# A fused attention and feed-forward kernel: a score tile that waits for two more exponentials, and a planner that keeps TensorE in attention for work that is nearly ready

## The chip, the cores and the metric

The kernel runs on one core of a Trainium2 chip. The metric is the device time of one execution in microseconds (us), less is better. Three runs of the kernel before took 1133.21, 1135.22 and 1140.99 us, so its median is 1135.22.

Names used below: PE is TensorE (matmuls), DVE is VectorE, ACT is ScalarE, POOL is GpSimd, SP is the engine that issues most of the DMAs (transfers).

## The reference

Block-causal attention over q, k and v (8 batches, 8 heads, 576 positions of 64 features, blocks of 64 positions), then a feed-forward net without an activation function: two projections, multiplied element by element, and a third one.

```python
scores = q @ k.T / sqrt(64)                 # [576, 576] of each head
scores = where(row_block >= column_block, scores, -1e9)
attn = exp(scores - rowmax);  attn /= attn.sum() + 1e-09
x = heads side by side of (attn @ v)        # 4608 tokens x 512
out = ((x @ w_a) * (x @ w_b)) @ w_out       # 512 -> 1536 -> 512
```

All of it is in 32-bit floats. The later part of the kernel and the attention of most heads make a product of 32-bit precision out of three products of a rounded part and a rest ("hi" and "lo").

## The kernel before, in words

**Stages.** Attention works on 32 pairs of heads (pair p, counted from 0; four pairs make a batch). While the pairs run, the first third of the feed-forward net (hidden blocks 0 to 3) is computed for the batches that are done, so that PE has work where attention waits for other engines. Then come the last batch's share of that first third (function `rest`), and at last the other two thirds for all tokens (lines from 1077 on, matmuls of L1160), with weights that DVE and ACT convert meanwhile.

**One pair.** The steps carry names that recur below.
- `lk`, `lq`, `lv`: SP loads k, q and v. From pair 10 on, `kh` and `qh` (ACT, L512 and L504) round k and q to a hi part, `kl` (POOL) and `ql` (DVE, L508) make the rest. Pairs 0 to 9 use the plain 32-bit matmul.
- Scores: there are four tiles of 128 query rows, numbered 3, 2, 1, 0, and a "side" tile of the first and last block of keys. `C3` writes tile 3 into bank pair x (128x512 for each of the two heads). `C1` writes the side tile (128x128) and tile 1 (128x320) into bank pair y. `C2` writes tile 2 (128x448) into x again, when tile 3's exponentials `e3` have read x. `C0` writes tile 0 (128x192) into y again, when `e4` (the side tile) and `e1` (tile 1) have read y. All of them are matmuls of L542, on halves of the array (64 rows of weights).
- DVE masks and takes row maxima (`m`, `t` with the tile's number: L576 to L580 and L568), ACT takes the exponentials (`e`, L595), two a tile, one for each head.
- `rc` sums and inverts (DVE), `N` scales (POOL, L683), `T` transposes on DVE (L688, L693); pairs 0 to 5 transpose on PE instead (L709). `D`, 16 small DMAs (L739), gathers the transposed probabilities into the tile `at`. `V0` to `V3` multiply them by v (L748), `X` copies the result out of PSUM, `H` and `S` split it into hi and lo for the feed-forward net, which can start on a batch when its four pairs have got that far.
- The next pair's `C3` needs x, so it waits for `e2`; its `C1` needs y, so it waits for `e0`.

**What sets the order.** None of this is issued in the order in which it is written. Each step is an `Op` with an engine, a list of steps that it needs, a key (its due time) and a cost from the table `TOOK`. The function `plan` plays the engines through these costs, and at each turn takes the ready step with the lowest key; the instructions are then recorded in the order that came out, and every engine works through its own list in that order. The feed-forward work is cut into groups of four matmuls (`mm4`, 128x288 each) with the highest key, so it fills what attention leaves. Each step of PE has a mode: 0 for whole-array work (feed-forward groups, transposes), 1 for scores, 2 for the values. A step whose mode isn't that of the step before it costs the planner `SWITCH` more. `SLACK` (0.3 us) is added where PE waits for another engine. The second third of the work is planned by a second call of `plan`, whose steps all have mode 0.

Of the kernel before, what the change touches and what calls it, by code (L numbers as in the profile page):

```python
# [35 lines left out]
K2 = 2  # L36
FIRST = 8
WARM_P = 2
PET = 6
A_KEY = 12  # L40
SLOTS = [12.0] * 12 + [15.2] * 20
CONV_AT = [0, 6.8, 13.6, 20.4, 28.2, 36, 43.8, 51.6, 59.4, 67.2, 75, 82.8]
CONV_KEY = 12.0
CONV_LO = True
KEEP_UNTIL, KEEP_EVERY = 66.0, 2.5
SWITCH = 0.1
LAGS = {"PE": 0.24, "DVE": 0.14, "Activation": 0.17, "Pool": 0.1, "SP": 2.0}
TOOK = {
# [41 lines left out]
def attention_then_bilinear_ffn(  # L90
# [272 lines left out]
    PE_, DVE_, ACT_, POOL_, SP_ = LAGS  # L363
# [12 lines left out]
    def plan(look=0.0):  # L376
        free = dict.fromkeys(LAGS, 0.0)
        ready = {e: [] for e in LAGS}
        users = [[] for _ in ops]
        left = [len(o.deps) for o in ops]  # L380
        for o in ops:
            for d, plus in o.deps:
                users[d.n].append((o, plus))
            if not o.deps:
                ready[o.eng].append(o)
        out = []
        mode = 0
        bus = 0.0
        held = []

        def since(o):
            if not o.frees:
                return o.at
            if len(held) < MM:
                return o.at
            r = held[-MM]
            return o.at if r is o else 1e9 if r.end is None else max(o.at, r.end)

        while any(ready.values()):
            t, e = min((max(free[e], min(map(since, q))), e) for e, q in ready.items() if q)  # L400
            o = min((o for o in ready[e] if since(o) <= t + look), key=lambda o: (o.key, o.n))
            t = max(t, since(o))
            if o.frees:
                held.append(o.frees)
            ready[e].remove(o)
            free[e] = t + o.took + (SWITCH if e == PE_ and o.mode != mode else 0)
            if e == PE_:
                mode = o.mode
            if o.also:
                free[ACT_] = max(free[ACT_], t) + o.also  # L410
            o.start, o.end = t, free[e] + o.lag
            if o.kind in KB:
                bus = max(bus, t + LATENCY - 0.3) + KB[o.kind] / RATE
                o.end = bus + 0.3
            out.append(o)
            for u, plus in users[o.n]:
                u.at = max(u.at, o.end + plus + (SLACK if u.eng == PE_ and e != PE_ else 0))
                left[u.n] -= 1
                if not left[u.n]:
                    ready[u.eng].append(u)  # L420
        assert len(out) == len(ops)
        return out
# [40 lines left out]
    def attention(p):  # L463
# [90 lines left out]

        def c1():
            y = bank("y")
            scores(NT, y[:, :, side])
            scores(1, y[:, :, :nk[1]])

        add("C3", PE_, lambda: scores(LAST, bank("x")), [("ql", p), ("kl", p), ("e3" if single_next else "e2", p - 1)], 0, at=B0, mode=1, kind=nat + "C3")  # L560
        add("C1", PE_, c1, [("C3", p, -LAGS[PE_]), ("ql2", p), *([("e4", p - 1), ("e1", p - 1)] if single_next else [("e0", p - 1)])], 0.1, mode=1, kind=nat + "C1")
# [58 lines left out]
        if single:  # L620
            c1_ = ("C1", p, -LAGS[PE_])
            r2 = Op("none", PE_, lambda: ring(2, 0), [(got("C1", p), -LAGS[PE_])], key=B0 + K2)

            def c2():
                ring(2, 1)
                scores(2, [view(2, h) for h in range(2)])

            o2 = add("C2", PE_, c2, [(r2, 0.0), c1_], K2 + .01, mode=1, kind=nat + "C2")
            def c0():
                ring(0, 1)  # L630
                st[0, 0] = ps_sc.tile([P, 512], F32, tag="av", name=f"s{n}_0_0")
                scores(0, [view(0, h) for h in range(2)])

            o0 = add("C0", PE_, c0, [("C2", p, -LAGS[PE_]), ("X", p - 1)], K2 + .1, mode=1, kind=nat + "C0")
            add("t2", DVE_, lambda: [nc.vector.tensor_reduce(st["nm"][:, h, 2:3], view(2, h), axis=AX.X, op=ALU.max, negate=True) for h in range(2)], [("C2", p), ("t3", p)], K2 + 1, kind="u2")
            add("t0", DVE_, lambda: [nc.vector.tensor_reduce(st["nm"][:, h, :1], view(0, h), axis=AX.X, op=ALU.max, negate=True) for h in range(2)], [("C0", p), ("t3", p)], K2 + 1.2, kind="u0")
        else:
            add("C2", PE_, lambda: scores(2, bank("x")[:, :, :nk[2]]), [("e3", p), ("C1", p, -LAGS[PE_])], 7.0, mode=1, kind=nat + "C2")
            add("C0", PE_, lambda: scores(0, bank("y")[:, :, :nk[0]]),
                [("C2", p, -LAGS[PE_]), ("e1", p), ("e4", p)], 7.1, mode=1, kind=nat + "C0")  # L640
            if masked:
                done["m2", p] = got("C2", p)
            else:
                add("m2", DVE_, lambda: mask(2, "x"), [("C2", p)], 8.0)
            add("t2", DVE_, lambda: top(2, st["x"][:, :, :nk[2]]), [("m2", p)], 8.1)
            if masked:
                done["m0", p] = got("C0", p)
            else:
                add("m0", DVE_, lambda: mask(0, "y"), [("C0", p)], 8.2)
            add("t0", DVE_, lambda: top(0, st["y"][:, :, :nk[0]]), [("m0", p)], 8.3)  # L650
# [907 lines left out]
```

## Time and profile before

| | |
|---|---|
| median of 3 runs | 1135.22 us (1133.21 to 1140.99) |
| span of the profiled execution, first to last instruction | 1131.4 us |
| what the median has above that span | 3.8 us |
| PE, DVE, ACT, POOL busy | 1106.5, 867.4, 634.7, 407.0 us |
| attention with the feed-forward work among it | from 0 to some 540 us of the span |

The profiled execution's own time is not among the three; its span is known, and 3.8 us stands for what lies around it.

In the page, a row of a group gives line, engine, operation, the tile written and the tiles read, shape, count, and then busy time and the mean of one instruction. In the rows of the timeline, the first number is the start in us from the span's start, the second the time that the merged instructions took, then engine, line, operation and tiles; square brackets hold the idle time before them and what ended it. A matmul's own time is longer than its distance to the next one, since matmuls are pipelined: what a step of PE costs is read from one start to the next.

### The profile page before, as it was taken

Reading aid. Unit: us, or ns where it says so; the run is one execution under the profiler, and the core shown is the slowest. Engines: PE = TensorE matmul, PEld = TensorE weight load, DVE = VectorE, ACT = ScalarE, POOL = GpSimd, SP = SyncE. Lnnn points to the kernel's source line nnn. Section 1 sums busy time; section 2 is a strip of 40 time slices with the busy share of each in tenths; the row PEclk is TensorE's granted clock in tenths of the full one; section 3 lists DMA queues with packets and bytes.
Section 4 is the critical chain, followed back from the end, with each engine's and each line's share of the span. In section 5 each row is a group of like instructions: output and inputs, shape, how many; then the busy total and the mean of one; then the engine's idle time right before and its main releaser. Section 6 shows DMA issues by size and latency. Waiting matters only on the chain.

```text
span 1131.4 us, 23204 instructions
## 1 busy us (share of the span) xinstructions
PE 1106.5 (98%) x8441; PEld 1040.2 (92%) x8441; DVE 867.4 (77%) x1797; ACT 634.7 (56%) x1632; POOL 407.0 (36%) x602
## 2 busy tenths in 40 slices
PE   8899999999999999999999999999999999999998
PEld 5567888899989998999999999999999999999998
DVE  6877878687678777753999997787874867867857
ACT  6877576566666556643465554545543545545532
POOL 4876667566656667551100120211202112022020
PEclk9999999999999999999999999999999999999999
DMA  5542688888777877857242663845669135055151
GB/s 171 156 145 87 168 242 217 226 227 213 205 222 210 223 210 201 240 159 209 90 146 73 181 179 86 215 121 144 181 217 333 37 76 112 17 96 102 26 98 56
DMA packets 78257, 178.74 MB, mean 158 GB/s; under 512 B 13120, under 2 KB 34624, under 8 KB 78144
## 3 DMA queue, kind: packets, MB, share of 16 engines
q1 hardware_dynamic: 65472, 159.95, 47.2%
q0 software_dynamic: 12672, 17.31, 10.2%
q8 instruction: 67, 1.10, 0.4%
q14 instruction: 46, 0.38, 0.1%
HBM read 80.74 MB, written 48.76 MB: 114 GB/s over the span
## 4 chain that ended last, share of the span: by engine, by line
PE 78%; DVE 6%; DMA 5%; ACT 4%; POOL 3%; SPq 3%; issue 2%; DVEq 0%; ACTq 0%; POOLq 0%
PE bank L1160 47%; PE ps L261 13%; PE pso L261 6%; PE av L748 5%; PE x L542 3%; PE y L542 2%; SPq L739 2%; ACT e L595 2%; POOL e L683 1%; DMA at<-bl 1%; DVE bl L688 1%; DMA qr<-qT 1%; DVE nm L568 1%; PE tp L709 1%; DMA kr<-kT 1%
## 5 line engine op out<-in xcount | busy, mean ns | idle before, releaser
L1160 PE MATMUL bank<-xh,wab 128*128 128x384 f32 x1344 | 350.0, 338 | 0.7 <-DVE t L1077 0.7
L1266 POOL DMA_DIRECT2D outT<-pt x88 | 78.0, 1129 | 468.6 <-ACT pt L1413 277.6
L1160 PEld LDWEIGHTS bank<-xh,wab 128*128 128x128 f32 x1344 | 244.7, 187 | 1.4 <-DVE t L1077 1.0
L1160 PE MATMUL bank<-xl,wab 128*128 128x384 f32 x672 | 227.0, 338 | 0.0
L261 PE MATMUL ps<-xh,wab 128*128 128x288 f32 x1024 | 213.9, 298 | 0.4 <-ACT ob L873 0.3
L261 PEld LDWEIGHTS ps<-xh,wab 128*128 128x128 f32 x1024 | 165.8, 188 | 6.4 <-issue 4.3
L683 POOL TENSOR_SCALAR e<-e,rc 128x512 f32<-128x512 f32 (+3 forms) x256 | 152.7, 616 | 45.3 <-DVE rc L663 45.3
L261 PE MATMUL ps<-xl,wab 128*128 128x288 f32 x512 | 153.3, 299 | 0.0
L1160 PEld LDWEIGHTS bank<-xl,wab 128*128 128x128 f32 x672 | 125.9, 187 | 0.0
L1077 DVE TENSOR_TENSOR u<-bank,u 128x384 f32<-128x384 f32 x156 | 86.7, 556 | 48.4 <-PE bank L1160 45.2
L688 DVE STREAM_TRANSPOSE bl<-e 128x512 f32<-128x512 f32 (+1 forms) x208 | 110.2, 582 | 10.4 <-POOL e L683 8.7
L1160 PE MATMUL bank<-hz,wo 128*128 128x384 f32 x612 | 110.0, 334 | 0.0
L1160 PEld LDWEIGHTS bank<-hz,wo 128*128 128x128 f32 x612 | 106.5, 188 | 0.0
L748 PEld LDWEIGHTS av<-at,v 128*64 128x64 f32 x1920 | 92.2, 137 | 10.3 <-issue 5.0
L748 PE MATMUL av<-at,v 128*64 128x128 f32 (+1 forms) x1920 | 97.2, 258 | 3.9 <-DMA at<-bl 2.7
L261 PE MATMUL pso<-hh,wo 128*128 128x288 f32 x480 | 100.9, 298 | 0.0
L261 PEld LDWEIGHTS ps<-xl,wab 128*128 128x128 f32 x512 | 96.1, 188 | 3.8 <-issue 3.2
L1077 DVE TENSOR_TENSOR t<-bank,t 128x384 f32<-128x384 f32 x96 | 53.3, 556 | 40.5 <-ACT t L1203 20.3
L261 PEld LDWEIGHTS pso<-hh,wo 128*128 128x128 f32 x480 | 77.6, 188 | 4.4 <-issue 4.1
L595 ACT ACTIVATE e<-y,nm 128x320 f32<-128x320 f32 (+1 forms) x126 | 60.9, 487 | 28.3 <-DVE nm L568 22.4
L568 DVE TENSOR_REDUCE nm<-x 128x2 f32<-128x1024 f32 (+1 forms) x63 | 72.1, 1145 | 5.7 <-PE x L542 4.5
L849 POOL TENSOR_TENSOR hl<-hf,hh 128x288 fp32r<-128x288 f32 x56 | 46.2, 825 | 84.0 <-ACT hh L845 81.6
(156 smaller groups left out, 2006.6 us busy)
## 6 DMA issues: line engine op xcount, KB each, us to landing
at<-bl SPq DMA_DIRECT2D x416, 112.0 KB, 2.5
xr<-xd SPq DMA_DIRECT2D x48, 384.0 KB, 4.6
outT<-pt POOLq DMA_DIRECT2D x88, 192.0 KB, 6.4
cv<-wab SPq DMA_DIRECT2D x24, 512.0 KB, 5.5
v<-vm SPq DMA_DIRECT2D x32, 320.0 KB, 3.5
xd<-xf SPq DMA_DIRECT2D x32, 288.0 KB, 2.6
outT<-ob SPq DMA_DIRECT2D x64, 144.0 KB, 2.3
wabd<-st SPq DMA_DIRECT2D x8, 896.0 KB, 5.3
```

Of the source, the lines that this page charges most:

```text
L261: nc.tensor.matmul(ps, w_, d_, start=(i == 0), stop=(i == n - 1))
L542: nc.tensor.matmul(out[h] if isinstance(out, list) else out[:, h], qq[r, q0[t]:q0[t] + P], keys, start=j == 0, stop=j == len(qk) - 1 and n ...
L568: nc.vector.tensor_reduce(st["nm"][:, :, t], view, axis=AX.X, op=ALU.max, negate=True)
L595: nc.scalar.activation(out, src, AF.Exp, bias=bias, accum_out=sm[:, h, t, :1])
L683: nc.gpsimd.tensor_scalar(ev, ev, st["rc"][:, h, t:t + 1], 1.0, op0=ALU.mult, op1=ALU.mult)
L688: nc.vector.transpose(dst, es[h][t].rearrange("p (c g q) -> p c g q", g=NQ, q=QB))
L739: nc.sync.dma_start(st["at"][QB * g:QB * (g + 1), i], bl[QB * i:QB * (i + 1), g])
L748: nc.tensor.matmul(out[d], v[:, h, c], a[:, qs, h, e_], start=start, stop=stop, skip_group_check=True)
L849: nc.gpsimd.tensor_tensor(lo, box2["hf"], f32(hi), op=ALU.subtract)
L1077: return lambda: v.tensor_tensor(o, a, b, op=op)
L1160: nc.tensor.matmul(banks[bk], a, b, start=start and not i, stop=i == 3 * n - 1, skip_group_check=not start)
L1266: do("acc", POOL_, lambda: nc.gpsimd.dma_start(part[o * P:(o + 1) * P, ts], t, accum_op=ALU.add), [name], [("part", o, 2 * tt_ + j)], key= ...
```

## The change

Four things change, all of them in the attention's planning.
- `C2` of the pairs from 8 on (`JOIN`) also waits for `e1` and `e4`, which `C0` waits for already.
- While PE is in mode 1 or 2, `plan` first looks for a step of such a mode that is ready within 0.3 us (`STAY`), and takes it (and waits for it) rather than work of mode 0.
- `SWITCH`, the planner's cost of a change of mode, is 0.2 instead of 0.1.
- In `C1`, tile 1's products stand ahead of the side tile's.

(A fifth line only writes a pair of the first pair's dependencies in another form.)

```diff
+JOIN = 8
+STAY = 0.3
...
-SWITCH = 0.1
+SWITCH = 0.2
...
             t, e = min((max(free[e], min(map(since, q))), e) for e, q in ready.items() if q)
-            o = min((o for o in ready[e] if since(o) <= t + look), key=lambda o: (o.key, o.n))
+            stay = [o for o in ready[e] if o.mode and since(o) <= t + STAY] if e == PE_ and mode else []
+            o = min(stay or (o for o in ready[e] if since(o) <= t + look), key=lambda o: (o.key, o.n))
             t = max(t, since(o))
...
             y = bank("y")
+            scores(1, y[:, :, :nk[1]])
             scores(NT, y[:, :, side])
-            scores(1, y[:, :, :nk[1]])
...
-            o2 = add("C2", PE_, c2, [(r2, 0.0), c1_], K2 + .01, mode=1, kind=nat + "C2")
+            o2 = add("C2", PE_, c2, [r2, c1_], K2 + .01, mode=1, kind=nat + "C2")
...
-            add("C2", PE_, lambda: scores(2, bank("x")[:, :, :nk[2]]), [("e3", p), ("C1", p, -LAGS[PE_])], 7.0, mode=1, kind=nat + "C2")
+            add("C2", PE_, lambda: scores(2, bank("x")[:, :, :nk[2]]), [("e3", p), *([("e1", p), ("e4", p)] if p >= JOIN else []), ("C1", p, -LAGS[PE_])], 7.0, mode=1, kind=nat + "C2")
```

The lines that the change adds move the line numbers, by two up to the planner and by three behind it: what is L229 before is L231 after, L261 is L263, L508 is L511, L542 is L545, L568 is L571, L580 is L583, L748 is L751, L841 is L844 and L1077 is L1080.

**TensorE, pair 20 (fifth batch, first heads).** In these rows x is the bank pair that tile 2 goes to, y the one of tile 0, ps a bank of a feed-forward group, av the values of pair 18. Before:

```order
L261 MATMUL ps_3_0_3_4597<-xh_2_0_3452,wab_81 128x288
L542 MATMUL x_0_5_4606<-k_0_4281,q_0_4289 128x448 x6
L261 MATMUL ps_3_0_3_4597<-xl_2_0_3453,wab_81 128x288
L261 MATMUL ps_3_0_3_4597<-xh_2_0_3452,wab_81 128x288
L261 MATMUL ps_3_0_3_4597<-xh_4_0_3694,wab_81 128x288
L261 MATMUL ps_3_0_3_4597<-xl_4_0_3695,wab_81 128x288
L542 MATMUL y_0_5_4629<-k_0_4281,q_0_4289 128x192 x6
L748 MATMUL av_4_4638<-at_4_4369,v_4_4248 64x64 x2
```

After:

```order
L263 MATMUL ps_3_0_3_4593<-xh_6_0_3959,wab_81 128x288
L545 MATMUL x_0_5_4619<-k_0_4307,q_0_4311 128x448 x6
L545 MATMUL y_0_5_4629<-k_0_4307,q_0_4311 128x192 x6
L751 MATMUL av_4_4640<-at_4_4378,v_4_4295 64x64 x2
L751 MATMUL av_4_4639<-at_4_4378,v_4_4295 64x128 x8
```

The group of four feed-forward matmuls that stood between tile 2 and tile 0 now stands ahead of tile 2.

**VectorE, pair 15's last maxima (x and y are its tiles 2 and 0, MEMSET is the mask, TENSOR_REDUCE the maximum) and pair 16's `ql` (SCALAR_TENSOR_TENSOR).** Before:

```order
L580 MEMSET x_6_5_3358 64x2x64
L568 TENSOR_REDUCE nm_6_3230<-x_6_5_3358 128x2
L580 MEMSET y_6_5_3375 64x2x64
L568 TENSOR_REDUCE nm_6_3230<-y_6_5_3375 128x2
L508 SCALAR_TENSOR_TENSOR q_0_3323<-qr_0_3324,q_0_3323 128x640
```

After:

```order
L583 MEMSET x_6_5_3376 64x2x64
L511 SCALAR_TENSOR_TENSOR q_0_3307<-qr_0_3308,q_0_3307 128x640
L571 TENSOR_REDUCE nm_6_3259<-x_6_5_3376 128x2
L583 MEMSET y_6_5_3387 64x2x64
L571 TENSOR_REDUCE nm_6_3259<-y_6_5_3387 128x2
```

`ql`, which needs the next pair's q, has moved from behind both maxima to a place ahead of tile 2's.

**VectorE, behind the last pair (cv and wab are weights in conversion, hf the product of two projections of the last planned feed-forward groups, numbered 1_1, 1_2 and 1_3, xt and xr the tokens of the later stage, read back by DMA).** Before:

```order
L229 TENSOR_TENSOR wab_7989<-cv,wab_7989 128x512
L841 TENSOR_TENSOR hf_1_1_7887<-ps_6_1_1_7867,a_1_1_7872 128x288
L1077 TENSOR_TENSOR xt_7987<-xr_7984,xr_7983 128x384
L1077 TENSOR_TENSOR xr_7983<-xr_7983 128x384
L1077 TENSOR_TENSOR xt_7987<-xr_7984,xr_7983 128x384
L1077 TENSOR_TENSOR xt_7987<-xr_7984,xt_7987 128x384
L841 TENSOR_TENSOR hf_1_2_7921<-ps_6_1_2_7901,a_1_2_7906 128x288
```

After:

```order
L844 TENSOR_TENSOR hf_1_2_7921<-ps_6_1_2_7901,a_1_2_7906 128x288
L224 TENSOR_TENSOR cv<-cv 128x128
L229 TENSOR_TENSOR wab_7989<-cv,wab_7989 128x384
L192 TENSOR_SCALAR cv<-cv 128x512
L231 TENSOR_TENSOR wab_7989<-cv,wab_7989 128x512
L1080 TENSOR_TENSOR xt_7987<-xr_7984,xr_7983 128x384
L1080 TENSOR_TENSOR xr_7983<-xr_7983 128x384
L844 TENSOR_TENSOR hf_1_3_7953<-ps_6_1_3_7935,a_1_3_7940 128x288
```

Before, 1_2 (and, four more instructions later, 1_3) stood behind the work on xr; after, 1_1 and 1_2 stand ahead of it, and 1_3 behind two instructions of it.

## The prediction

> **What bounds the kernel now.** I read the page first, then busy time by stretches, then who PE waited for, then single steps of PE in the timeline. The page:
>
> ```profile
> span 1131.4 us, 23204 instructions
> PE 1106.5 (98%) x8441; PEld 1040.2 (92%) x8441; DVE 867.4 (77%) x1797; ACT 634.7 (56%) x1632; POOL 407.0 (36%) x602
> PE   8899999999999999999999999999999999999998
> PE 78%; DVE 6%; DMA 5%; ACT 4%; POOL 3%; SPq 3%; issue 2%; DVEq 0%; ACTq 0%; POOLq 0%
> ```
>
> PE is busy nearly all of the time and carries 78% of the chain that ended last; the nearest other engine, DVE, is at 77% busy. By stretches (core, then busy us of PE, PEld, DVE, ACT, POOL; the clock granted to PE comes after them):
>
> ```profile
> 0.00:120.00 120.00, 106.44 (x888) 77.35 (x889) 92.61 (x190) 90.05 (x270) 82.84 (x138) 0.97 0.43 138
> 120.00:500.00 380.00, 375.33 (x3782) 340.32 (x3781) 290.07 (x678) 239.32 (x766) 236.18 (x362) 1.00 0.78 214
> 500.00:540.00 40.00, 37.60 (x354) 36.69 (x353) 14.60 (x33) 12.39 (x30) 8.07 (x14) 1.00 0.68 198
> 540.00:1131.40 591.40, 587.07 (x3424) 585.88 (x3422) 470.10 (x900) 292.98 (x567) 79.87 (x90) 1.00 0.47 124
> ```
>
> The change touches the first three stretches, where attention and feed-forward groups share PE. The work there is fixed and PE is never without some for long, so a us that PE saves by another order is a us of the span, and a us of new waiting costs one. PE's idle time in 120 to 500 is 380 - 375.33 = 4.7 us, in 500 to 540 it is 2.4. So little is to be had from waits; what an order can save lies inside the busy time, at the borders between kinds of matmul. There a busy PE isn't a working one.
>
> **Price of a border.** Starts of PE in pair 20, where a feed-forward group stands between tile 2 (x, 448 columns) and tile 0 (y, 192 columns), and in pair 31, where none does:
>
> ```profile
> 314.35 0.87 PE L542 MATMUL x<-k,q 64*128 64x448 f32 x6
> 315.15 0.40 PE L261 MATMUL ps<-xl,wab 128*128 128x288 f32 x1
> 315.87 0.58 PE L542 MATMUL y<-k,q 64*128 64x192 f32 x6
> 316.38 0.45 PE L748 MATMUL av<-at,v 128*64 128x64 f32 x6
> ...
> 319.30 0.54 PE L261 MATMUL ps<-xh,wab 128*128 128x288 f32 x2
> ...
> 489.48 0.88 PE L542 MATMUL x<-k,q 64*128 64x448 f32 x6
> 490.18 0.49 PE L542 MATMUL y<-k,q 64*128 64x192 f32 x6
> 490.60 0.54 PE L261 MATMUL ps<-xh,wab 128*128 128x288 f32 x2
> ...
> 491.33 0.28 PE L748 MATMUL av<-at,v 128*64 128x64 f32 x2
> ```
>
> A feed-forward group by itself, inside a long stretch (the first and the last start of 8 matmuls, of which the rows between are left out):
>
> ```profile
> 335.78 0.42 PE L261 MATMUL pso<-hh,wo 128*128 128x288 f32 x2
> ...
> 336.83 0.29 PE L261 MATMUL pso<-hl,wo 128*128 128x288 f32 x1
> ```
>
> That is 1.05 us for eight, 0.13 a matmul, 0.53 a group of four. Apart, tile 2 takes 0.80 (314.35 to 315.15), the group 0.72, tile 0 0.51: 2.03, of which 0.53 is the group's own work, so 1.50. Together, tile 2 and tile 0 take 0.70 + 0.42 = 1.12. The two borders cost 0.38. Of that 0.72 - 0.53 = 0.19 shows in the group's stretch, and another 0.19 in the two tiles, which are shorter when they adjoin. The same holds for the first two steps, together in pair 21 and apart in pair 22:
>
> ```profile
> 306.09 0.96 PE L542 MATMUL x<-k,q 64*128 64x512 f32 x6
> 306.89 0.93 PE L542 MATMUL y<-k,q 64*128 64x128 f32 x12
> 307.75 0.40 PE L261 MATMUL ps<-xl,wab 128*128 128x288 f32 x1
> ...
> 337.05 0.96 PE L542 MATMUL x<-k,q 64*128 64x512 f32 x6
> 337.94 0.53 PE L261 MATMUL pso<-hh,wo 128*128 128x288 f32 x2
> 338.66 1.04 PE L542 MATMUL y<-k,q 64*128 64x128 f32 x12
> 339.63 0.40 PE L261 MATMUL pso<-hh,wo 128*128 128x288 f32 x1
> ```
>
> Together 1.66; apart 2.58 - 0.53 = 2.05: 0.39 for two borders. A group between tile 0 and values (490.60 to 491.33) takes 0.73, as between scores, so I take 0.195 for a border of any kind.
>
> **Sum of the borders.** I counted borders in the order of the two built programs, from pair 8's scores on. Tile 2 and tile 0 adjoin in 3 of 24 pairs before and in all 24 after; `C3` and `C1` adjoin in 21 before and in 16 after (a group has slipped in between); values follow scores directly at 20 places instead of 15. Stretches of feed-forward groups fall from 73 to 57, borders of all kinds from 170 to 138. 32 x 0.195 = 6.2 us saved. Before pair 8 there are some three stretches fewer, around transposes, whose borders no row prices well; PE waits there anyway, and I count nothing (0 to 0.6 us of gain).
>
> That every change of tile shape drains PE is what the Trainium skill says (TensorEngine Tiling (Array Packing), Key Properties), and TensorE: Matmul & The Clock Gate (Single matmul latency; Back-to-back issue gap) gives (398 + N) / 2.4 ns for a matmul alone against N / 2.4 + 2.5 in a stream, so a drain would cost about 163 ns and, as an estimate from that page, the 32 borders 5.2 us. The rows' 0.195 is a fifth more, and the measurement decides.
>
> Tile 1's products ahead of the side tile's: the same 12 matmuls into the same bank, nothing for PE. DVE's side maximum can start only when both are done, as before, since it waits for the whole step. The planner's larger `SWITCH` costs the chip nothing; it works through the order alone.
>
> **What waits more.** (1) `C2` for `e1` and `e4`. PE is in order, so all that is planned behind `C2` waits with it. The order puts 13 groups between `C1` and `C2` in pair 20 (12 before; over the 24 pairs the mean rises from 10.5 to 13.6). From `C1`'s start in 20, at 306.89, that is 0.86 + 13 x 0.53 + 0.2 = 7.95 us. The last of `e1` and `e4` there:
>
> ```profile
> 314.51 0.23 ACT L595 ACTIVATION_READ_ACCUMULATOR e_s<-y,nb 128x1 f32 x1
> ```
>
> 314.74 - 306.89 = 7.85. So it fits by 0.1: PE waits now and then. `C0` met that same wait before, with a like margin, so most of it only moves. I take +0.6 us (0 to 3).
>
> (2) The next `C3` for `e2`, the tighter one. Between `C2` and the next `C3` the groups fall from 6.1 to 2.8 in the mean, since they now stand ahead of `C2`. What is left is 1.12 (both tiles), 2.92 (values, 316.38 to 319.30) and one or two groups of 0.53 with their border: 4.8 to 5.3 us. How long `e2` takes from `C2`, in pair 31, where nothing is in its way, and in pair 20, where something is:
>
> ```profile
> 493.69 0.20 ACT L595 ACTIVATION_READ_ACCUMULATOR e<-x,nm 128x1 f32 x1
> ...
> 318.34 0.67 ACT L512 CAST k<-kr 128x576 fp32r<-128x576 f32 x1 [3.27 <-DMA kr<-kT]
> 321.22 0.19 ACT L595 ACTIVATION_READ_ACCUMULATOR e<-x,nm 128x1 f32 x1
> 321.47 0.96 PE L542 MATMUL x<-k,q 64*128 64x512 f32 x6 [1.36 <-ACT e L595]
> ```
>
> 493.89 - 489.48 = 4.4 clean; 321.41 - 314.35 = 7.1 with ACT held by the next pair's k, which had not landed. After the change `kh` and `qh` mostly stand further ahead of `e2` on ACT, which helps, but on DVE `ql` now stands ahead of tile 2's maximum in some pairs (pair 15 above) and between the two maxima in others: a late q then holds `e2` or `e0` itself. What PE waited in this way before (us in total, times, longest):
>
> ```profile
> PE x L542 <- ACT e L595: 2.6, 5, 1.4
> PE av L748 <- DMA at<-bl: 2.7, 3, 1.1
> ```
>
> I take twice the first row, +2.6 us, since twice as many pairs are now short of slack (0 if the casts are clear of it; 15 if a wait of pair 20's 1.36 comes in every second of 22 pairs). The second row, values that wait for their transfers, I leave as it is (1.3 either way).
>
> (3) Near 150 us the first batch's 60 groups are used up ahead of pair 7's values, where two were left before. The next group belongs to the second batch and needs pair 7's result, copied, cast and subtracted; only pair 10's `C3` and `C1` (1.66) stand between. The same chain of another pair, its first half:
>
> ```profile
> 494.66 0.62 ACT L767 COPY xf<-av 128x512 f32<-128x512 f32 x1
> 495.31 0.77 ACT L787 CAST xh<-xf 128x288 fp32r<-128x288 f32 x2
> 496.11 1.58 POOL L791 TENSOR_TENSOR xl<-xf,xh 128x288 fp32r<-128x288 f32 x2
> ```
>
> 496.11 + 0.79 - 494.66 = 2.2. So +0.6 us (0 to 1.9).
>
> (4) Behind the last pair. 19 groups follow its values instead of 29, so PE gets to `rest` 10 x 0.53 = 5.3 us sooner after them, while DVE still starts on xr 13 us after them:
>
> ```profile
> 519.78 2.87 PE L748 MATMUL av<-at,v 128*64 128x128 f32 x56 [1.14 <-DMA at<-bl]
> 535.55 0.56 DVE L1077 TENSOR_TENSOR xt<-xr,xr 128x384 f32<-128x384 f32 x1 [2.12 <-DMA xr<-xd]
> 555.19 0.46 DVE L285 TENSOR_TENSOR hf<-ps,a 128x288 f32<-128x288 f32 x1 [1.02 <-PE ps L261]
> 593.89 0.44 PE L1160 MATMUL bank<-xh,wab 128*128 128x384 f32 x1 [0.69 <-DVE t L1077]
> ```
>
> DVE is close to full from there to 594, where PE waits for it already. Its lead shrinks by up to 5.3; its own pauses on the way (1.02 at 555.19 is one for PE) and the banks of PSUM, which let PE run on, take most of that. +1.0 us (0 to 5).
>
> Sum: -6.2 + 0.6 + 2.6 + 0.6 + 1.0 = -1.4, a span of 1130.0 us. With the 3.8 us that the median has above the span: **1133.8**, said as 1133.5.
>
> **The rivals.** *Slower, through the maxima and `e2`.* The freed groups no longer cover `C2` to `C3`, and late loads of k and q hold the exponentials. For it: 4.4 against 4.8 to 5.3 leaves half a us, and pair 20 took 7.1. Against it: the casts have moved ahead. It decides from a mean wait of 6.2 / 22 = 0.28 us a pair; at 1.36 in every second pair it is -6.2 + 15 + 2.2 = +11, 1146; at half that, 1139. *DVE's lost lead comes back in full.* For it: the wait at 593.89 is there today; against it, the pause at 555.19, where DVE had caught up with PE. Then +5 instead of +1: 1138. *The change doesn't do what it says:* PE keeps to attention but stands idle up to 0.3 us for it, about what two borders save (0.39), and nothing is left: 1136. *The waits shrink instead:* casts early enough, no wait on `e2`, half of the waits on transfers gone: -6.2 - 2.6 - 1.3 = -10, 1125 to 1128 with the other terms.
>
> **How the numbers follow.** Forecast 0.45 (1130 to 1137), slower through `e2` 0.17, DVE's lead 0.13, nothing left 0.13, shrinking waits 0.12. The range reaches from the last rival's upper end to between the first rival's two times: 1126.5 to 1141. About 1% (11.4 us) is what a measurement of this kernel can tell from no change; its three runs lie 7.8 apart. Faster by that needs 1123.9, more than all borders and most waits together: 0.03. Slower by it needs 1146.6, the first rival in full: 0.05. Within: 0.92.
>
> **What would show it.** In the profile after: tile 2 to tile 0 at 0.70 and 0.42 everywhere from pair 8 on; the row of x waiting for ACT's e near 5 us instead of 2.6 (over 12: the first rival; near 0: the last); idle PE near 150 us of about 1; the wait on DVE's t near 590 of 1 to 3 us (5: the second). If tiles that adjoin cost what they cost apart, the sum of the borders is wrong.

## The result, and the profile after

The changed kernel takes 1150.28 us (median of four runs, 1147.37 to 1152.51), the kernel before took 1134.48 beside it (1133.21 to 1140.99). The ratio is 1.0116, with a 95% interval of 1.008 to 1.0153: slower, where 1133.5 was forecast and 1126.5 to 1141 was the range. (Two of the runs reported below, both of `STAY` alone, took 2135.85 and 5850.76 us and are left out of its ratio.)

The page of the changed kernel (span, busy engines, and the share of each engine in the chain that ended last):

```profile
span 1145.6 us, 23219 instructions
PE 1107.4 (97%) x8441; PEld 1049.6 (92%) x8441; DVE 864.0 (75%) x1797; ACT 633.1 (55%) x1632; POOL 404.5 (35%) x602
PE 71%; DVE 10%; ACT 6%; DMA 5%; POOL 4%; SPq 2%; issue 2%; ACTq 0%; DVEq 0%; POOLq 0%
```

PE's busy time is the same to 1 us (1106.5 before) in a span 14.2 us longer; what the borders saved and what a slower clock took, below, both hide in it. PE's share of the chain fell from 78% to 71%, and that of DVE rose from 6% to 10%, that of ACT from 4% to 6%. Where the time went, the stretches tell:

```profile
0.00:120.00 120.00, 105.10 (x866) 77.68 (x867) 86.90 (x180) 87.45 (x261) 82.20 (x134) 0.96 0.42 137
120.00:500.00 380.00, 361.87 (x3621) 334.36 (x3622) 280.07 (x658) 231.68 (x743) 222.89 (x348) 0.99 0.76 208
```

In 120 to 500 PE is idle for 380 - 361.87 = 18.1 us, where it was 4.7. It got through 3621 matmuls there instead of 3782. The wait list of PE, from 120 to 560 us, in the changed kernel:

```profile
PE x L545 <- ACT e L598: 10.3, 10, 1.9
PE y L545 <- ACT e L598: 3.4, 5, 1.0
PE av L751 <- DMA at<-bl: 2.4, 2, 1.4
PE x L545 <- POOL q L491: 1.6, 1, 1.6
```

The wait on exponentials, 2.6 us before, is 13.7 now. All fifteen of these waits stand ahead of `C3` (x) or `C1` (y), none ahead of `C2`, which is the step that got the new wait. Two of them, with tile 2 and tile 0 of pair 20 joined as the change wants it, the next pair's `C3` behind them, and pair 31's `C3`:

```profile
324.68 0.88 PE L545 MATMUL x<-k,q 64*128 64x448 f32 x6
325.38 0.49 PE L545 MATMUL y<-k,q 64*128 64x192 f32 x6
325.80 2.98 PE L751 MATMUL av<-at,v 128*64 128x64 f32 x60
...
331.10 0.96 PE L545 MATMUL x<-k,q 64*128 64x512 f32 x6 [1.06 <-ACT e L598]
...
496.70 0.96 PE L545 MATMUL x<-k,q 64*128 64x512 f32 x6 [1.84 <-ACT e L598]
```

Behind three of such waits, at 160.6, 365.4 and 498.6 us, the granted clock falls to half for 3.4 us, as it does at 14, 41 and 103 us (in the kernel before it did so twice, at 13 and 71 us, and never later). Two of them, each as the window ahead of the drop and the window of the drop; the number after POOL's is the clock:

```profile
362.00:365.40 3.40, 1.29 (x10) 0.68 (x10) 1.24 (x4) 3.40 (x13) 1.25 (x2) 1.00 0.81 193
365.40:368.80 3.40, 3.40 (x36) 3.28 (x36) 3.11 (x8) 0.04 (x1) 3.40 (x6) 0.51 0.62 149
495.20:498.60 3.40, 1.90 (x17) 1.34 (x19) 2.25 (x3) 3.24 (x12) 1.36 (x3) 0.99 0.79 186
498.60:502.00 3.40, 3.40 (x41) 3.40 (x38) 2.33 (x7) 0.21 (x1) 3.40 (x6) 0.50 0.67 155
```

The loss is complete when the second stage begins. Its first matmul, in the kernel before and in the changed one:

```profile
583.31 0.34 PE L1160 MATMUL bank<-xh,wab 128*128 128x384 f32 x1
```

```profile
596.67 0.34 PE L1163 MATMUL bank<-xh,wab 128*128 128x384 f32 x1
```

That is 13.4 later; the rest takes 548.1 us before and 548.9 after. To split the 13.4 I took, for each two kinds of steps that follow each other, the usual distance of their starts (the 30th percentile over both kernels). What lies more than 0.12 us above it is a wait, and what is above it in a half-clock window is the clock's. By this count waits rose by 13.8 us (24.9 to 38.7), the clock's part by 8.7 (2.6 to 11.3), and the work itself fell by 9.3, as the joined tiles were to bring (over all pairs there are 35 borders fewer, 6.8 us at 0.195; the count gives 2.5 more than that). The count is rough. Four drops more, each 3.4 us at half clock, can take 4 x 1.7 = 6.8 us at most, so some 2 us of the 8.7 are waits that fall into those windows.

### The profile page after: what moved, and what is told of

Same layout as the page of the kernel before. It is cut to its first block, busy times and chain, and to the rows that moved or that the text cites. A ratio compares the mean times of both kernels' runs of the same rounds, so it can differ in the third digit from the quotient of the medians.

```text
span 1145.6 us, 23219 instructions
## 1 busy us (share of the span) xinstructions
PE 1107.4 (97%) x8441; PEld 1049.6 (92%) x8441; DVE 864.0 (75%) x1797; ACT 633.1 (55%) x1632; POOL 404.5 (35%) x602
## 4 chain that ended last, share of the span: by engine, by line
PE 71%; DVE 10%; ACT 6%; DMA 5%; POOL 4%; SPq 2%; issue 2%; ACTq 0%; DVEq 0%; POOLq 0%
PE bank L1163 47%; PE ps L263 9%; PE pso L263 6%; PE av L751 4%; DMA qr<-qT 4%; ACT e L598 3%; PE x L545 2%; POOL e L686 2%; PE y L545 2%; SPq L742 2%; DVE nm L571 2%; DVE bl L691 1%; ACT at L718 1%; POOL xl L794 1%; DVE q L511 1%
## 5 line engine op out<-in xcount | busy, mean ns | idle before, releaser
L1269 POOL DMA_DIRECT2D outT<-pt x88 | 77.9, 1128 | 469.8 <-ACT pt L1416 278.3
L263 PE MATMUL ps<-xh,wab 128*128 128x288 f32 x1024 | 216.0, 301 | 0.1
L263 PEld LDWEIGHTS ps<-xh,wab 128*128 128x128 f32 x1024 | 167.4, 190 | 5.2 <-issue 2.1
L263 PE MATMUL ps<-xl,wab 128*128 128x288 f32 x512 | 153.1, 299 | 0.0
L1080 DVE TENSOR_TENSOR u<-bank,u 128x384 f32<-128x384 f32 x156 | 86.7, 556 | 48.6 <-PE bank L1163 45.5
L691 DVE STREAM_TRANSPOSE bl<-e 128x512 f32<-128x512 f32 (+1 forms) x208 | 111.5, 584 | 12.1 <-POOL e L686 7.0
L751 PEld LDWEIGHTS av<-at,v 128*64 128x64 f32 x1920 | 94.4, 140 | 8.4 <-issue 3.6
L751 PE MATMUL av<-at,v 128*64 128x128 f32 (+1 forms) x1920 | 99.3, 262 | 2.6 <-DMA at<-bl 2.4
L263 PE MATMUL pso<-hh,wo 128*128 128x288 f32 x480 | 99.9, 297 | 0.0
L263 PEld LDWEIGHTS ps<-xl,wab 128*128 128x128 f32 x512 | 97.1, 190 | 1.1 <-issue 0.4
L1080 DVE TENSOR_TENSOR t<-bank,t 128x384 f32<-128x384 f32 x96 | 53.3, 556 | 40.4 <-ACT t L1206 20.3
L571 DVE TENSOR_REDUCE nm<-x 128x2 f32<-128x1024 f32 (+1 forms) x63 | 71.7, 1138 | 11.0 <-PE x L545 10.2
L263 PEld LDWEIGHTS pso<-hh,wo 128*128 128x128 f32 x480 | 77.7, 188 | 1.2 <-issue 0.4
L545 PE MATMUL x<-k,q 64*128 64x512 f32 (+1 forms) x340 | 62.1, 464 | 14.5 <-ACT e L598 10.3
```

The lines of the kernel that those rows point to most:

```text
L263: nc.tensor.matmul(ps, w_, d_, start=(i == 0), stop=(i == n - 1))
L545: nc.tensor.matmul(out[h] if isinstance(out, list) else out[:, h], qq[r, q0[t]:q0[t] + P], keys, start=j == 0, stop=j == len(qk) - 1 and n ...
L571: nc.vector.tensor_reduce(st["nm"][:, :, t], view, axis=AX.X, op=ALU.max, negate=True)
L691: nc.vector.transpose(dst, es[h][t].rearrange("p (c g q) -> p c g q", g=NQ, q=QB))
L751: nc.tensor.matmul(out[d], v[:, h, c], a[:, qs, h, e_], start=start, stop=stop, skip_group_check=True)
L1080: return lambda: v.tensor_tensor(o, a, b, op=op)
```

## The experiments

Sixteen kernels ran. Each has the changed kernel or the kernel before as its base and alters a number or a rule or two.

**First: which part of the change.** Of the two theories in the expectations, W blames the added wait, E the planner's settings in the early pairs.

The changed kernel without the added wait:

```diff
-JOIN = 8
+JOIN = 99
```

> The changed kernel without its added wait (tile 2 waits for tile 3's exponentials alone, as before); the planner's two new settings and the order inside the second step stay. Tile 2 and tile 0 adjoin in 8 of 24 pairs, 6.6 groups stand between tile 2 and the next pair's first step. Theory W (the added wait takes the cover from the next pair's first step, so PE waits for exponentials, and the clock halves after such waits): most of the loss goes, 1130 to 1137 us, PE's wait for exponentials back at 2 to 4 us, at most two or three halved stretches of the clock. Theory E (the planner's settings spoil the early pairs, where the changed kernel is 6 us behind by the time the 50th feed-forward group starts): 1141 or more, still some 6 us behind at that group.

1160.2 us, ratio 1.0212 [1.0178, 1.0246]: worse still, where theory W had 1130 to 1137. So the added wait isn't the cause; beside the other parts it makes the loss smaller. Alone, in the kernel before (with `SWITCH` at 0.1, no `STAY`, and tile 1 in its old place):

```diff
+JOIN = 8
...
-            add("C2", ..., [("e3", p), ("C1", p, -LAGS[PE_])], ...)
+            add("C2", ..., [("e3", p), *([("e1", p), ("e4", p)] if p >= JOIN else []), ("C1", p, -LAGS[PE_])], ...)
```

> The kernel before with the added wait alone (from pair 8 on tile 2 waits for tile 1's and the side tile's exponentials too). Tile 2 and tile 0 adjoin in all 24 pairs, 3.6 groups between tile 2 and the next pair's first step, 4 groups behind the last pair's values. Theory W: slow, 1143 to 1153, PE waits 8 to 12 us for exponentials in the scores' lines, four or more halved stretches. Theory E: 1131 to 1138, since the early pairs are as before.

1138.13 us, 1.0014 [0.9992, 1.0037]: the time stays, though this order has 27 borders fewer (143 from pair 8 on), worth 5.3 us at 0.195. So the wait does cost something, and the borders pay for it. The changed kernel without the `STAY` rule:

```diff
-            stay = [o for o in ready[e] if ...] if e == PE_ and mode else []
+            stay = [o for o in ready[e] if ...] if e == PE_ and mode and STAY else []
...
-STAY = 0.3
+STAY = 0.0
```

> The changed kernel without the planner's rule to keep PE in attention for work soon ready; the added wait, the doubled cost of a change of mode and the order in the second step stay. The steps of pairs 8 on stand nearly as in the changed kernel (2.6 groups between tile 2 and the next first step). Theory W: 1145 to 1153, as the changed kernel. Theory E: 1136 to 1143, the 50th group 3 us sooner or more, if it is the rule that spoils the early pairs.

1148.0 us, 1.0116 [1.0076, 1.0155], as the changed kernel, and a miss for theory E (1136 to 1143), which had about fitted the two runs before it. And the kernel before with tile 1's products first:

```diff
-            scores(NT, y[:, :, side])
             scores(1, y[:, :, :nk[1]])
+            scores(NT, y[:, :, side])
```

> The kernel before with tile 1's products ahead of the side tile's, nothing else; all engines' orders are otherwise the same. Both theories: no change, 1132 to 1138. If it is over 1140, the order of the products inside the second step costs something of its own.

1135.1 us, 1.0001 [0.9981, 1.0021]. What all slow kernels have in common by now is `SWITCH = 0.2`, the one part that the prediction had set at nothing.

**Second: `SWITCH` alone.** The kernel before with that number:

```diff
-SWITCH = 0.1
+SWITCH = 0.2
```

> The kernel before with the planner's SWITCH at 0.2 instead of 0.1 and nothing else of the change. Theory S (the larger SWITCH alone is the cause: with 0.1 the plan thinks TensorE earlier than it comes, so that operands are ready when it does; with 0.2 the plan's pace is the chip's and that cushion is gone, so late loads of k and q and late exponentials stop TensorE and its clock halves in places): 1146 to 1160 us, idle TensorE of 12 us or more between 160 and 500 us, three or more drops of the clock after 120 us. Rival J (SWITCH is harmless by itself, and only STAY, the added wait and SWITCH together make the slow order): 1133 to 1139 us, with the idle time of the kernel before (about 5 us between 120 and 500).

1157.15 us, 1.0199 [1.0136, 1.0263]. Its stretch from 120 to 500 us, and the first row of its waits:

```profile
120.00:500.00 380.00, 359.86 (x3536) 323.30 (x3535) 280.44 (x659) 226.68 (x727) 223.35 (x345) 0.99 0.75 208
```

```profile
PE x L542 <- ACT e L595: 12.0, 14, 2.4
```

Its order looks harmless: 163 borders from pair 8 on instead of 170, 10.3 groups between tile 1 and tile 2 instead of 10.5, 5.8 between tile 2 and the next pair instead of 6.1. The reverse, the changed kernel with the old number:

```diff
-SWITCH = 0.2
+SWITCH = 0.1
```

> The changed kernel with SWITCH back at 0.1: the added wait, STAY and tile 1 first stay. Theory S: the loss goes, 1130 to 1139 us, no drop of the clock after 160 us or one. Rival J (the grouped order as such is the cause, tile 2 joined to tile 0 in all 24 pairs and the groups gone from between tile 2 and the next pair): 1146 to 1152 us, since those stay (24 joined, 3.0 groups against 2.8 in the changed kernel).

1136.53 us, 1.0015 [0.9991, 1.0039]. The added wait, `STAY` and tile 1's place together leave the time as it was (what their 28 borders fewer save is spent on waits and behind the last pair); the larger `SWITCH` is the whole loss. `STAY` alone in the kernel before:

```diff
+STAY = 0.3
...
-            o = min((o for o in ready[e] if since(o) <= t + look), key=lambda o: (o.key, o.n))
+            stay = [o for o in ready[e] if o.mode and since(o) <= t + STAY] if e == PE_ and mode else []
+            o = min(stay or (o for o in ready[e] if since(o) <= t + look), key=lambda o: (o.key, o.n))
```

> The kernel before with the STAY rule alone (TensorE stays in attention for work that is ready within 0.3 us). It has 148 borders from pair 8 on instead of 170. Theory S: the cushion is left, and the 22 borders at 0.195 us are worth 4.3 us: 1130 to 1136 us. Rival J: STAY is part of what spoils the order: 1138 to 1148 us.

1135.32 us, 0.9992 [0.9962, 1.0022]: its 22 borders fewer, 4.3 us by the price, brought nothing that can be measured (by the count above waits were 28.5 us in its profile instead of 24.9). Then an attempt to give the changed kernel a cushion by another number:

```diff
-SLACK = 0.3
+SLACK = 0.6
```

> The changed kernel with SLACK at 0.6 instead of 0.3: the plan lets TensorE take a step 0.6 us after its operands by plan, not 0.3, so a cushion is put back by another number, with SWITCH at 0.2 and all the rest of the change. Theory S, in its form that the cushion is what counts: 1132 to 1143 us, with idle TensorE between 160 and 500 us at 10 us or less (20 in the run without the added wait). If S holds only for some other work of SWITCH: 1146 to 1155 us.

1156.28 us, 1.0183 [1.0132, 1.0235]: a miss, and the theory had to say more exactly what the cushion is.

**What `SWITCH` does.** The planner keeps the start that it gives to each step. Pair 24 in the kernel before, from `C3` to `C2`, with the last of the exponentials for which `C2` waits:

```profile
368.60 0.96 PE L542 MATMUL x<-k,q 64*128 64x512 f32 x6
...
375.92 0.23 ACT L595 ACTIVATION_READ_ACCUMULATOR e<-x,nb 128x1 f32 x1
...
376.81 0.87 PE L542 MATMUL x<-k,q 64*128 64x448 f32 x6
```

And with `SWITCH` at 0.2:

```profile
371.03 0.96 PE L542 MATMUL x<-k,q 64*128 64x512 f32 x6
...
379.09 0.23 ACT L595 ACTIVATION_READ_ACCUMULATOR e<-x,nb 128x1 f32 x1
...
379.37 0.87 PE L542 MATMUL x<-k,q 64*128 64x448 f32 x6 [0.66 <-ACT e L595]
```

Before, PE had 8.21 us of work between the two (the plan thought 8.03), and the exponential was there after 7.55: 0.66 us to spare. With the larger `SWITCH` the plan again counts on more than enough, 8.75 us, but 0.91 of them are time in which the plan lets PE stand; the four borders at 0.2 the chip takes as well. The chip's work there is 379.37 - 0.66 - 371.03 = 7.68 us, the exponential is there after 8.29, and PE waits. The exponential is later too, by 0.74 us: in the new order `ql` stands ahead of tile 3's maximum on DVE, and a copy of values between the two exponentials on ACT. Each wait is covered by work which the planner counts out to fit, by its own costs. Where the plan's PE is slower than the chip's, too little work is counted out. Where it is faster, there is more than needed, and that surplus can cover exponentials, loads and casts that come later than planned. This is the reading that the next runs try; one pair doesn't show it.

From pair 10's `C3` to pair 31's values the plan's time goes from 348.7 us (before) to 366.9 (`SWITCH` alone). The chip's work for it, its time less waits and clock, is the same: 360.3 and 360.7. I call the difference the lead of the plan: 11.6 us before, -6.2 with `SWITCH` at 0.2. The 17.8 us between the two are, to within 1 us, the price of the borders, 154 x 0.1 = 15.4, and 3.0 of longer pauses of the plan's PE (3.3 instead of 0.3). The price of a border in the plan has come nearer to the chip's 0.195, and the plan got worse by it. The old price alone would have made a lead of 154 x 0.095 = 14.6, so the plan's other prices were some 3 us too high already.

**Third: is it the pace?** The changed kernel, `SWITCH` still at 0.2, with feed-forward steps planned too short:

```diff
-"mm4": (0.528, 0.24, 0)
+"mm4": (0.48, 0.24, 0)
```

> The changed kernel with one more number of the planner altered: a feed-forward step of four matmuls is planned at 0.48 us instead of 0.528; SWITCH stays at 0.2. Theory P (pace: what counts is by how much the plan's TensorE is faster than the chip's; it is the only cushion that the exponentials have, and the larger SWITCH took it away): 13.6 steps between tile 1 and tile 2, each planned 0.048 us too short, give 0.65 us of cushion back, so the waits on exponentials shrink to those of the kernel with SWITCH at 0.1 and the time falls to 1130 to 1139 us, though SWITCH is still 0.2. If SWITCH spoils the order in another way than by the pace: 1146 to 1156 us.

1138.5 us, 1.0011 [0.9983, 1.004]: the loss is gone with `SWITCH` untouched. The same stretch and the waits on exponentials there (in one of its faster runs, 1132.78 us):

```profile
120.00:500.00 380.00, 372.57 (x3775) 349.16 (x3775) 284.41 (x667) 236.78 (x752) 231.75 (x356) 1.00 0.77 211
```

```profile
PE x L545 <- ACT e L598: 4.0, 2, 2.9
PE y L545 <- ACT e L598: 3.4, 3, 1.3
```

That is 7.4 us instead of the changed kernel's 13.7.

The other way round, the kernel before with nothing of the change, and feed-forward steps planned too long:

```diff
-"mm4": (0.528, 0.24, 0)
+"mm4": (0.55, 0.24, 0)
```

> The kernel before, with nothing of the change, but a feed-forward step of four matmuls planned at 0.55 us instead of 0.528. Theory P: the plan's TensorE is slower by 10.5 x 0.022 = 0.23 us between tile 1 and tile 2 (SWITCH at 0.2 makes it slower by about 0.3 there), so most of the cushion goes and the time rises to 1143 to 1156 us. If the pace isn't the cause: 1134 to 1139 us.

1149.37 us, 1.0123 [1.0086, 1.016], the loss of the changed kernel without any line of it. PE's idle time from 120 to 500 is 14 us:

```profile
120.00:500.00 380.00, 366.04 (x3593) 327.23 (x3592) 288.38 (x672) 231.04 (x743) 228.10 (x349) 1.00 0.76 209
```

For the clock's part, the changed kernel with work put into two of its waits (the numbers in `FILL` are those of the feed-forward steps ahead of `C3` in pairs 23 and 31):

```diff
+FILL = {2128: 3, 2998: 3}
...
-                nc.tensor.matmul(ps, w_, d_, start=(i == 0), stop=(i == n - 1))
+                for z in range(1 + extra[0]):
+                    nc.tensor.matmul(ps, w_, d_, start=(i == 0 and z == 0), stop=(i == n - 1 and z == extra[0]))
...
         for o in plan():
+            extra[0] = FILL.get(o.n, 0)
             o.fn()
```

> The changed kernel, with the feed-forward step just ahead of tile 3 of pairs 23 and 31 issued four times over instead of once (12 matmuls more at each place, 1.6 us; the sums that they add to come out wrong, all else is the reference's). TensorE waited 1.7 and 1.9 us at these two places and its clock fell to half right behind each. Theory C (the clock falls where TensorE was busy for less than about 1.95 of 3.41 us): the work fills the waits and costs nothing, no drop of the clock behind the two places, 3 to 5 us less than the changed kernel: 1145 to 1148 us. If the clock falls for another reason, or the waits only move: the drops stay and the time is 1150 to 1153 us.

1151.37 us, 1.0122 [1.0087, 1.0157], beside 1.0116 for the changed kernel. In the profiled run the drops behind the two places are gone; at the first:

```profile
362.00:365.40 3.40, 2.69 (x25) 1.91 (x23) 1.20 (x5) 2.73 (x11) 1.96 (x3) 1.00 0.76 174
365.40:368.80 3.40, 3.40 (x65) 3.33 (x64) 3.04 (x9) 0.07 (x1) 3.40 (x6) 1.00 0.83 175
```

The drop at 160.6 is gone as well, though nothing was added there, and a new one stands at 464. So a single profile shows only in part what the filling did. Nor does the median settle what the drops cost, since the four runs differ in their clocks:

| filled kernel, us | 1146.71 (profiled) | 1150.60 | 1152.13 | 1153.20 |
|---|---|---|---|---|
| granted clock, mean | 0.995 | 0.994 | 0.989 | 0.989 |

The changed kernel had 0.990 to 0.991 in all four. So in two of the four filled runs the clock was no better than without the filling, and the run with the best clock lies in theory C's 1145 to 1148. In the ten runs of the kernel with steps of 0.48 the two also go together: 1131.84 and 1133.97 us at 0.997, 1140.63 and 1141.87 at 0.991. A run with longer waits can have both the lower clock and the longer time, so this doesn't show either that the clock adds to the waits. What its part is worth stays open.

The fourth of these runs went for fewer borders and more lead at once, `SWITCH` at 0.1 and steps at 0.50:

```diff
-SWITCH = 0.2
+SWITCH = 0.1
...
-"mm4": (0.528, 0.24, 0)
+"mm4": (0.50, 0.24, 0)
```

> The changed kernel with SWITCH back at 0.1 and the feed-forward step planned at 0.50 us: 130 borders from pair 8 on against 170 in the kernel before (40 x 0.195 = 7.8 us saved), and more cushion than the changed kernel with SWITCH at 0.1 alone. Theory P: waits after 120 us no more than in the kernel before, and as no feed-forward step is left behind the last values, VectorE's lead is gone, about 3.4 us lost in the second stage: 1129 to 1135 us. If the cushion doesn't come from the pace: 1136 us or more, as with SWITCH alone.

1144.33 us, 1.0074 [1.0047, 1.0101]: a miss. With it the pace was in doubt, and the next four were to decide.

**Fourth: pace or luck.** The kernel before with `SWITCH` at 0.2 (1157 us) and the pace given back:

```diff
-SWITCH = 0.1
+SWITCH = 0.2
...
-"mm4": (0.528, 0.24, 0)
+"mm4": (0.50, 0.24, 0)
```

> The kernel before with SWITCH at 0.2 (1157 us by itself) and a feed-forward step planned at 0.50 us instead of 0.528, without the added wait, STAY or the order of tile 1. Theory P: 11.5 steps x 0.028 = 0.32 us between tile 1 and tile 2 give back what the three borders there took (3 x 0.1), so the pace is that of the kernel before: 1133 to 1142 us. Rival L (no pace is at work, each altered number only deals another order, good or bad by chance, as the run with SWITCH at 0.1 and steps of 0.50 us suggests): anywhere from 1134 to 1158 us, more likely 1145 or more, as three of the four kernels with SWITCH at 0.2 and one other number altered were.

1141.59 us, 1.0038 [1.0012, 1.0063]: most of the loss of 1.0199 is back. The changed kernel at half the dose:

```diff
-SWITCH = 0.2
+SWITCH = 0.15
```

> The changed kernel with SWITCH at 0.15. Theory P: half of the cushion that SWITCH took is back, so the time lies between the changed kernel (1150) and the one with SWITCH at 0.1 (1136.5): 1139 to 1147 us. Rival L: no order between the three.

1146.56 us, 1.0085 [1.0058, 1.0111]: between 1150.3 and 1136.5. The step between the run that fitted and the one that didn't:

```diff
-SWITCH = 0.2
+SWITCH = 0.1
...
-"mm4": (0.528, 0.24, 0)
+"mm4": (0.515, 0.24, 0)
```

> The changed kernel with SWITCH at 0.1 and a feed-forward step planned at 0.515 us, between the run at 0.528 (1136.5) and the one at 0.50 (1144.3), where VectorE's transposes stood ahead of tile 1's maximum in all pairs and tile 0 waited in every fourth. Theory P with that accident apart: transposes stand ahead of it in fewer pairs here, so 1132 to 1139 us. If more pace is itself harmful from here on: 1139 to 1144 us.

1136.02 us, 0.999 [0.9969, 1.0011]. And the version meant to beat both, the kernel before with the `STAY` rule and

```diff
-"mm4": (0.528, 0.24, 0)
+"mm4": (0.515, 0.24, 0)
```

> A version meant to beat both: the kernel before with the STAY rule alone, SWITCH at 0.1, and a feed-forward step planned at 0.515 us: 151 borders from pair 8 on against 170 (19 x 0.195 = 3.7 us saved), a cushion 11 x 0.013 = 0.14 us larger between tile 1 and tile 2, and 20 feed-forward steps left behind the last values (19 cost 0.8 us in the changed kernel). Theory P: 1130 to 1135 us, a ratio of 0.995 to 1.000. Rival L: 1136 to 1148 us.

1134.03 us, 0.998 [0.9962, 0.9998]: 0.2% below the kernel before, by an interval that only just leaves out no difference.

All four came out in the range that the pace had given them. Rival L allowed for 1141.59 as well, and for 1146.56 between its neighbours by chance; 1134.03 lies outside its 1136 to 1148. In the table, the lead of the plan and what waits and clock took, both from pair 10's `C3` to pair 31's values, by the rough count above and from one profile each (not in it are tile 1 first, which has the plan of the kernel before, and the filled kernel, which has the plan of the changed one):

| kernel | plan, us | chip's work | lead | waits + clock | ratio to before |
|---|---|---|---|---|---|
| `STAY`, 0.515 | 348.5 | 362.7 | +14.2 | 8.8 | 0.998 |
| before | 348.7 | 360.3 | +11.6 | 6.7 | 1 |
| changed, 0.48 | 359.0 | 367.7 | +8.7 | 5.1 | 1.0011 |
| added wait alone | 361.5 | 369.1 | +7.7 | 14.7 | 1.0014 |
| `STAY` alone | 349.4 | 356.7 | +7.4 | 11.0 | 0.9992 |
| `SWITCH` 0.2, 0.50 | 352.5 | 359.7 | +7.2 | 11.1 | 1.0038 |
| changed, `SWITCH` 0.1 | 363.9 | 370.1 | +6.2 | 12.1 | 1.0015 |
| before, 0.55 | 358.8 | 361.6 | +2.8 | 18.8 | 1.0123 |
| changed, 0.1, 0.515 | 365.6 | 367.5 | +1.9 | 15.8 | 0.999 |
| changed, `SWITCH` 0.15 | 368.2 | 368.6 | +0.4 | 18.0 | 1.0085 |
| changed, 0.1, 0.50 | 366.8 | 365.5 | -1.3 | 21.0 | 1.0074 |
| changed without `STAY` | 360.6 | 354.8 | -5.8 | 23.0 | 1.0116 |
| `SWITCH` 0.2 alone | 366.9 | 360.7 | -6.2 | 26.9 | 1.0199 |
| changed without added wait | 365.1 | 358.4 | -6.7 | 31.3 | 1.0212 |
| `SLACK` 0.6 | 376.7 | 369.1 | -7.7 | 22.9 | 1.0183 |
| changed | 365.0 | 357.1 | -7.8 | 22.3 | 1.0116 |

Kernels with a lead above 6 us lose 5 to 15 us to waits and clock, those below 3 lose 16 to 31. Single profiles scatter, though: with tile 1 first, the plan being that of the kernel before, PE was idle in 120 to 500 for 10.3 us instead of 4.7, in a run 4 us above its median:

```profile
120.00:500.00 380.00, 369.73 (x3721) 336.18 (x3721) 287.87 (x673) 234.68 (x753) 229.74 (x356) 1.00 0.77 211
```

The lead fits the miss at 0.50. With `SWITCH` 0.1 and steps of 0.50 the plan has used up all 432 feed-forward steps that it can put there, and lets PE stand for 19.1 us (0.3 in the kernel before); the chip has no such pauses, so the lead is gone though each step is planned short. (The expectation of the run at 0.515 blames VectorE's transposes for the same miss; nothing tests that apart.)

`SLACK` isn't cleared up by it. Its plan is the longest, 376.7 us, but PE stands for only 4.3 of them; the rest is feed-forward work, for which the chip takes 369.1 instead of 357.1, so the lead is that of the changed kernel, -7.7. Why 0.3 us more at every wait, most of it filled with work, covered nothing stays open.

Nor do the times follow the lead line by line. The run at 0.515 with `SWITCH` at 0.1, where the plan's pauses are 10.8 us, is the plain exception: lead +1.9 and 0.999, beside +2.8 and 1.0123 for the kernel before with steps of 0.55. Of the 13 us between these two, 38 borders (135 and 173 from pair 8 on) account for 7.4 and waits and clock for 3.0.

I formed this measure after the runs; what was forecast from the pace and came out are the runs at 0.48, 0.55, 0.15, and 0.50 with `SWITCH` at 0.2. That `SWITCH` is the cause is shown both ways; that it works through the pace rests on these four forecasts, with `SLACK` against it and the single order worth some us either way.

## Why the prediction was wrong

**The step that failed** is the sentence that the planner's larger `SWITCH` "costs the chip nothing; it works through the order alone". It does work through the order alone, but I looked in the order for borders and for groups ahead of each wait, and took the differences between tiles as all there is. I never asked how well the plan's PE keeps time with the chip's, although every cover in this order is counted out by the plan's clock. The two numbers for it stood in the prediction: I measured a border at 0.195 us and read that the plan charges 0.1. What follows, that the plan's PE had been fast by 0.095 x 154 = 14.6 us at its borders from pair 10 on, and that the change takes that away, I didn't draw. In place of nothing it costs 21 us by itself (`SWITCH` alone), of which the rest of the change gets about 6 back.

**Borders: right.** Tile 2 and tile 0 adjoin at 0.70 and 0.42 (324.68, 325.38, 325.80). The price holds too: the changed kernel with `SWITCH` at 0.1 has 28 borders fewer than before, 5.5 us at 0.195. Its second stage starts 1.2 us earlier, with waits up by 2.3 and the clock's part by 1.8; so its work was 5.3 us less, by the rough count.

**(1) `C2` for `e1` and `e4`: right in the changed kernel, too cheap alone.** +0.6 was taken, and in the changed kernel `C2` isn't among the steps that wait for an exponential. But the kernel with the added wait alone comes out 0.14% slower (from -0.08 to 0.37%) with 5.3 us of borders saved, so the wait and what it moves cost it some 7 us, at other steps than `C2`.

**(2) The next `C3` for `e2`: right place, wrong size.** 5 us were forecast in the row of x waiting for e, 10.3 came, and 3.4 more in the row of y that I had no line for. I put the risk on the 2.8 groups left behind `C2`, but without the added wait 6.6 groups stand there and the row of x still has 9.8, and the kernel with `SWITCH` at 0.1 has 3.0 groups and stays at 6.8 (with tile 1 first, in the old order, one run had 5.8):

```profile
PE x L545 <- ACT e L598: 6.8, 11, 1.1
PE y L545 <- ACT e L598: 1.6, 1, 1.6
```

So the first rival (1139 to 1146 us) had the sign and the symptom. Its mechanism, freed groups that no longer cover `C2` to `C3`, isn't the main cause, and even its full price fell short.

**(3) Near 150 us: too small.** 0.6 us (0 to 1.9) were allowed; two `C3` wait there, and the second pulls the clock down behind it:

```profile
143.82 1.13 PE L545 MATMUL x<-k,q 64*128 64x512 f32 x4 [1.65 <-POOL q L491]
...
158.92 0.97 PE L545 MATMUL x<-k,q 64*128 64x512 f32 x6 [1.89 <-ACT e L598]
```

3.5 us in two waits, where before there was one of 0.20. Only the second, behind pair 7's values, is at the place that the term was about; the first waits for pair 9's q.

**(4) DVE's lead: right.** +1.0 forecast with 19 groups left behind the last values; from the second stage's start to the end it is 548.9 instead of 548.1, +0.8. Where no group is left (`SWITCH` at 0.1; steps of 0.48) it is 551.6 and 551.5, and a new wait is seen there:

```profile
PE bank L1163 <- DVE xl L1115: 2.0, 2, 1.2
```

That is why the kernel with steps of 0.48, whose second stage starts at 579.47, 3.8 us ahead of the kernel before, ends no sooner.

**The clock** was in no term. It fell four more times by the profile, which can cost 6.8 us at most. The run with filled waits doesn't settle how much of that comes on top of the waits; a rival that doubles its waits should have named it.

**The chances:** 0.05 for slower by over 1% came from one rival in full. No case held a cause that works on all waits at once. (The range's lower end, 1126.5, lies inside the last rival's 1125 to 1128, not at its upper end, as the prediction has it; that decided nothing.)

## What to carry to other kernels

Where an order is planned with costs, a cost that is too low on the bottleneck engine can be a cushion that helps to hold the order together: correct it only together with the other costs and margins, and compare the plan's total time with the chip's work, which a trace of the kernel before already gives. Here a lead above 6 us went with few waits and one below 3 with many. A margin set by another number need not do the same: `SLACK` at 0.6 gave none. And of a change in several parts, a number that "only" steers a planner is the first to test by itself.

## What was not expected of the hardware

The clock doesn't need an idle window to fall. In the changed kernel it fell to half behind windows of 3.4 us in which PE was busy for 1.29 and 1.90 us (rows above), and with 2.69 us of work in the same place it stayed. The edge isn't sharp. With `SWITCH` at 0.1 and steps of 0.50, a window with 2.12 us was followed by a drop:

```profile
343.60:347.00 3.40, 2.12 (x20) 1.36 (x19) 2.09 (x7) 3.18 (x12) 2.89 (x5) 1.00 0.22 63
347.00:350.40 3.40, 3.21 (x34) 3.19 (x34) 3.04 (x5) 0.71 (x3) 0.60 (x1) 0.51 0.52 118
```

In the filled kernel, one with 1.88 us was not:

```profile
153.70:157.10 3.40, 1.88 (x42) 1.74 (x38) 2.58 (x4) 1.36 (x6) 2.39 (x3) 1.00 0.77 183
157.10:160.50 3.40, 2.73 (x24) 2.17 (x25) 1.69 (x5) 2.24 (x8) 1.41 (x2) 1.00 0.80 219
```

The Trainium skill (TensorE: Matmul & The Clock Gate, What's actually happening) has the clock at half "after ≥1 idle window (~3.4µs)"; the 3.4 us agree with these rows, the idle window doesn't.
